# Another order of the steps in a fused layernorm, linear attention and Mish feed-forward kernel

## The chip, the cores and the metric

The kernel runs on one core of a Trainium2 chip. The metric is the device time of one execution in microseconds (us). A core has TensorE (PE, with its weight loads as PEld), VectorE (DVE), ScalarE (ACT), GpSimd (POOL) and SyncE (SP), each with its own instruction stream, and 16 DMA engines that work off what the queues of SP and ACT issue. All times below are in us from the start of the span unless another unit stands there.

## The reference

```python
x  = A_x                                   # [1, 2048, 448], bf16
xn = layernorm(x)                          # eps 1e-5, no scale or shift
# attention part, H = 16 heads of 28
q, k, v = heads(xn @ wqkv)                 # wqkv [448, 3*448]
pq = q @ w_phi[h];  pk = k @ w_phi[h]      # w_phi [16, 28, 28]
phi_q = concat(softmax(pq), softmax(-pq))  # 56 features a head
phi_k = concat(softmax(pk), softmax(-pk))
kv = phi_k^T v;   z = sum over tokens of phi_k
o  = (phi_q kv) / (phi_q z + 1e-6)
# feed-forward part, F = 1792
h   = xn @ w1 + b1
act = h * tanh(softplus(h))                # Mish
out = x + o @ wo + act @ w2
```

All tokens see the same kv and z, so no output of the attention part can be made before k and v of all tokens are done.

## The kernel before

Tokens are tiled 16 tiles of 128; tiles 2u and 2u+1 form pair u (u = 0 to 7). Almost all matmuls take 64 rows and run two at a time in the two halves of TensorE, one for each tile of a pair; each piece of such work is cut into a part 1 (8 matmuls of a projection) and a part 2 (6), which swap the halves.

The stages are these.

- *Weights of the feature maps.* Wq and Wk are loaded transposed, with one transposing DMA each (`lqT`, `lkT`, line 285), and their last 64 rows are copied once (`qda`, `kdd`). w_phi is loaded in two parts (line 301): 384 of its 448 rows (`lp0`) and the other 64 (`lp1`). POOL multiplies them with a mask into a block-diagonal Wbd (`bd`, line 547): the first two of three multiplies read the large part, the third the small one. PE multiplies WqT and WkT with Wbd (`wmq0` to `wmq3`, `wmk0` to `wmk3`, line 563), which gives the weights Wpq and Wpk that make pq and pk directly from xn. Each such group reads all of Wbd.
- *Layernorm.* Statistics of a tile on DVE (`st..d`, lines 468 and 469) or ACT (`st..a`, lines 460 to 464); rstd of a pair on ACT (`rs..a`, Ln and Exp, lines 481 and 483) or POOL (`rs..p`, lines 474 and 477); xn of a pair on DVE (`xn..d`, line 502) or POOL (`xn..p`, with a small shift on DVE, lines 490 and 497). Then xn is transposed on PE (`xt..a`, `xt..d`, `xt..b`, line 510) with the copy out of PSUM on ACT, DVE or half on each, or by a transposing DMA on SP's queue (`xt..m`, line 522). Such a DMA waits for xn of its pair, and for tiles 0 and 15 of x.
- *Projections.* `q`, `k`, `v` of each pair on PE (line 439). ACT makes exp of both signs from q (line 653) and k (line 592); v is copied by DVE or ACT (lines 517, 515). exp of q goes to one of three buffers (pair modulo 3) and is transposed per tile by DMA (`e0` to `e15`, line 661). exp of k is summed and inverted on DVE and normalised on POOL (`kn`, lines 600 to 604).
- *Key-value state.* `kv0` to `kv7` on PE (line 621) sum over all pairs; `kvz` on DVE (line 633) adds eps and masks with `mask2`, which POOL makes (`pk`, lines 351 to 360), and one transposing DMA hands it on as KVZ.
- *Feed-forward.* `f0.c` and `f1.c` are the two halves of the tokens for 14 blocks c of F; PE (line 439), then Mish on ACT (line 672), into rows of actT. The products with W2 are `G` in halves and `g` whole (lines 835, 797).
- *Output.* `nd` of a tile on PE (line 695), numerators and denominators on DVE (lines 710 to 721), the pair transposed by DMA (`ot..m`, line 730), and the product with Wo (`wo`, lines 835, 813). Both output products of a pair add up in the same two banks of PSUM; DVE adds x (line 762), SP stores (`sto`, `stt`).

What sets the order is one list of step names, ORDER. Each step appends its instructions to the streams of the engines it uses, in the order of the list; what an instruction must wait for is derived from what it reads and writes. So the list fixes the order on every engine and every queue, the bank of PSUM that a step gets, and, by a letter at the end of a name, the engine: a for ACT, d for DVE, p for POOL, s for SP's queue, m for a DMA, b for both.

```python
for name in order:
    steps[name]()
```

A load of x has `load_x(a, b, eng)` behind it: `x1` loads tiles 2 and 3, `x2` 4 and 5, `t6` and `t7` one tile, `x4` tiles 8 to 11, `x6` 12 to 15, `x0` 0 and 1. `lvm`, `ly0`, `ly1` load Wv, `l1m0` to `l1m2`, `lz0`, `lz1` W1, `l2` W2, `lo` Wo, `lb` b1. `z16` is 16 matmuls on constants ahead of everything on PE, `table` loads ACT's table, `pp`, `pi`, `pm`, `pv` are constants on POOL.

Of the kernel before, what the change touches and what calls it, by code (L numbers as in the profile page):

```python
# [146 lines left out]


ORDER = """
lp0a pp2 z16 lx1s pi pk st3d pp1 lqT lkT table lx2a pp0 pm lp1a st2d lba bd st4a rs1p st5d lx4a qda rs2a b1 xn1d wmq3a  # L150
xn2d lt6s lx0s wmq1a kdd wmq2a wmq0a xt1b xt2d wmk3a ly0s st6d lt7s st7d st9d wmk2a lvms wmk0a ly1s wmk1a q11 lx6s rs3a
xn3d q21 st8d st14d q12 rs4p xt3m q22 v21d st0d k21 xn4p st15d rs7p l1m2s e3 v11d v22a st11d v12a k22 st10d k11 st12d
xn7d v31d st13d xt4m st1d k12 k31 l1m0s pv q31 v32d rs0p e2 xt7m rs5a xn0d k32 k41 xn5d q32 e4 v41d k42 rs6p q41 xt0m
v42d xn6d k71 q42 k72 xt5m l1m1s v71a e6 xt6m kn2.1 v01a k01 lz0a v02d v72d kn1.1 k51 kn4.1 k02 e7 v51a k52 e5 lz1s k61
kn3.1 v52d kn1.0 k62 l2s q51 q61 q52 kn7.1 q62 f0.11 v61a f1.31 v62a e11 kn5.0 f0.12 kn6.1 f1.21 f1.11 f1.32 e12 e8
f1.22 kn6.0 kn0.1 f0.21 f1.12 e13 ep f0.22 f1.51 e10 f1.01 f0.121 f1.02 kv6 kv1 kn2.0 kn4.0 f0.122 f1.52 los f0.51 kn3.0
f0.71 kn7.0 f0.52 e9 f0.72 kn0.0 q71 q01 q72 q02 f0.101 kv2 kn5.1 kv0 kv7 e1 kv5 kv4 kv3 f1.61 kvz f0.102 e14 f1.121
f1.62 f1.122 f0.131 f0.61 f0.132 f0.31 e15 f1.71 f0.62 f0.32 f0.81 e0 f1.72 nd2 f0.82 f0.111 f0.01 f0.112 f0.41 nd3
f0.02 f0.42 f1.81 nd1 f0.91 ot1m f1.82 f0.92 f1.101 nd7 f1.91 f1.102 G11 nd0 f1.41 wo11 f1.92 nd6 G12 f1.111 wo12 f1.112
ot0m f1.42 ot3m nd5 G31 nd10 nd4 G01 wo32 G02 wo31 nd11 f1.131 G32 f1.132 ot5m nd14 ot2m wo01 G21 wo52 nd15 wo22 wo51  # L160
wo02 ot7m wob nd12 G51 wo21 nd13 G52 ot6m G42 sto1 G22 G41 sto0 nd9 nd8 wo61 G61 wo7F g14 G62 sto2 ot4m wo41 wo62 wo7H
sto3 wo42 sto5 stt14 sto4 sto6 g15 stt15
"""


# [816 lines left out]
```

## Time and profile before

| | us |
|---|---|
| three runs | 151.71, 152.47, 152.88 |
| median | 152.47 |
| profiled execution | 151.52 |
| its span, first to last instruction | 149.7 |
| PE busy | 144.5 |
| DVE busy | 103.0 |
| ACT busy | 71.6 |
| POOL busy | 38.7 |

The granted clock of TensorE was 1.0 over the whole span. The profile's busy rows show how much of each of 40 equal slices (3.7 us) an engine worked, in tenths. The chain of waits follows the work that ended last back from the end: what each piece waited for, or the piece before it on its engine. A row of the timeline has start, length, engine, line, operation, what it writes and reads, and how many instructions are merged into it; in brackets, how long the engine stood idle before it and what ended that. The rows of SPq and ACTq are the issues of DMAs; their landing times are in the view of the DMAs and of a tile. Times of merged rows reach from the first start to the last end.

### The profile page before, as it was taken

Reading aid. Unit: us, or ns where it says so; the run is one execution under the profiler, and the core shown is the slowest. Engines: PE = TensorE matmul, PEld = TensorE weight load, DVE = VectorE, ACT = ScalarE, POOL = GpSimd, SP = SyncE. Lnnn points to the kernel's source line nnn. Section 1 sums busy time; section 2 is a strip of 40 time slices with the busy share of each in tenths; the row PEclk is TensorE's granted clock in tenths of the full one; section 3 lists DMA queues with packets and bytes.
Section 4 is the critical chain, followed back from the end, with each engine's and each line's share of the span. In section 5 each row is a group of like instructions: output and inputs, shape, how many; then the busy total and the mean of one; then the engine's idle time right before and its main releaser. Section 6 shows DMA issues by size and latency. Waiting matters only on the chain.

```text
span 149.7 us, 3958 instructions
## 1 busy us (share of the span) xinstructions
PE 144.5 (97%) x1719; PEld 76.0 (51%) x1719; DVE 103.0 (69%) x228; ACT 71.6 (48%) x88; POOL 38.7 (26%) x55
## 2 busy tenths in 40 slices
PE   7989999799999999999999999999999999999991
PEld 2375554456555554744444455555555555554451
DVE  0689985849999992020179979799787996387072
ACT  3688989938999578986765612410020000000000
POOL 6800832044999999200000000000000000000000
PEclk9999999999999999999999999999999999999999
DMA  4994899999999990079300302300032112400604
GB/s 132 272 330 136 185 246 199 133 283 195 294 222 234 244 123 0 4 138 145 72 0 4 61 4 47 75 4 0 4 70 59 25 36 52 166 36 0 184 30 154
DMA packets 41484, 17.23 MB, mean 115 GB/s; under 512 B 35708, under 2 KB 40700, under 8 KB 41468
## 3 DMA queue, kind: packets, MB, share of 16 engines
q1 hardware_dynamic: 40448, 15.95, 50.6%
q10 hardware_dynamic: 1020, 1.04, 2.2%
q8 instruction: 13, 0.21, 0.6%
q14 instruction: 3, 0.02, 0.0%
HBM read 6.57 MB, written 1.84 MB: 56 GB/s over the span
## 4 chain that ended last, share of the span: by engine, by line
PE 86%; DMA 6%; DVE 3%; issue 1%; POOL 1%; ACT 0%; ACTq 0%
PE PS L439 45%; PE PS L835 31%; DMA xnT<-xn 3%; PE PS L797 3%; DMA Wraw<-in_A_w_phi_dram 3%; PE PS L695 2%; PE PS L621 2%; DVE xn L502 2%; PE PS L813 1%; PE PS L563 1%; POOL rstd L477 0%; PE PS L510 0%; DVE x_all L762 0%; ACT L317 0%; ACTq L301 0%
## 5 line engine op out<-in xcount | busy, mean ns | idle before, releaser
L439 PE MATMUL PS<-xnT,W 64*128 64x512 bf16 x392 | 45.0, 376 | 0.0
L672 ACT ACTIVATE actT<-PS,b1T 128x1024 bf16<-128x1024 f32 x28 | 29.9, 1112 | 30.7 <-PE PS L439 30.7
L835 PE MATMUL PS<-W,actT 64*128 64x448 bf16 x392 | 38.9, 349 | 0.0
L439 PEld LDWEIGHTS PS<-xnT,W 64*128 64x128 bf16 x392 | 19.2, 94 | 20.3 <-ACT actT L672 0.5
L604 POOL TENSOR_TENSOR actT<-actT,rSk 128x896 bf16<-128x896 bf16 x16 | 26.6, 1698 | 10.4 <-DVE rSk L602 10.4
L835 PEld LDWEIGHTS PS<-W,actT 64*128 64x128 bf16 x392 | 18.3, 94 | 17.7 <-issue 0.4
L600 DVE TENSOR_REDUCE Sk<-actT 128x32 f32<-128x896 bf16 x16 | 16.6, 1040 | 0.0
L762 DVE TENSOR_TENSOR x_all<-PS,x_all 128x448 bf16<-128x448 f32 (+1 forms) x16 | 9.1, 613 | 9.1 <-PE PS L835 8.7
L592 ACT ACTIVATE actT<-PS 128x896 bf16<-128x896 f32 x16 | 13.6, 929 | 3.4 <-PE PS L439 3.4
L710 DVE COPY Sq<-PS 128x16 f32<-128x16 f32 x32 | 4.0, 166 | 15.2 <-PE PS L695 15.2
L439 PE MATMUL PS<-Wv,xnT 64*128 64x448 bf16 x112 | 12.8, 349 | 0.8 <-DMA xnT<-xn 0.8
L439 PE MATMUL PS<-Wpk,xnT 64*128 64x448 bf16 x112 | 12.5, 349 | 0.0
L439 PE MATMUL PS<-Wpq,xnT 64*128 64x448 bf16 x112 | 11.8, 349 | 0.0
L468 DVE BATCH_NORM_STATS2 stats<-x_all 128x6 f32<-128x448 bf16 x15 | 9.1, 607 | 3.6 <-DMA x_all<-in_A_x_dram 3.5
L718 DVE TENSOR_TENSOR v_all<-v_all 128x464 f32<-128x464 f32 x16 | 10.3, 642 | 0.6
L714 DVE TENSOR_TENSOR v_all<-PS,Sq 128x464 f32<-128x464 f32 x16 | 10.3, 642 | 0.5
L721 DVE TENSOR_TENSOR xn<-v_all,rden 128x448 bf16<-128x448 f32 x16 | 10.0, 625 | 0.6
L716 DVE TENSOR_TENSOR v_all<-PS,Sq 128x464 f32<-128x464 f32 x16 | 10.1, 629 | 0.0
L653 ACT ACTIVATE actT<-PS 128x896 bf16<-128x896 f32 x10 | 8.5, 918 | 0.9 <-PE PS L439 0.9
L439 PEld LDWEIGHTS PS<-Wv,xnT 64*128 64x128 bf16 x112 | 5.8, 94 | 5.8 <-DVE rSk L602 1.2
L517 DVE CAST v_all<-PS 128x896 bf16<-128x896 f32 x5 | 5.3, 1077 | 4.7 <-PE PS L439 4.7
L439 PEld LDWEIGHTS PS<-Wpk,xnT 64*128 64x128 bf16 x112 | 5.9, 94 | 4.8 <-issue 0.3
(86 smaller groups left out, 123.9 us busy)
## 6 DMA issues: line engine op xcount, KB each, us to landing
W<-in_B_w_dram SPq DMA_DIRECT2D x1, 1568.0 KB, 8.8
out_dram<-x_all SPq DMA_DIRECT2D x7, 224.0 KB, 2.2
W<-in_B_w_dram SPq DMA_DIRECT2D x3, 448.0 KB, 4.1
Wo<-in_A_wo_dram SPq DMA_DIRECT2D x2, 336.0 KB, 3.4
x_all<-in_A_x_dram SPq DMA_DIRECT2D x2, 224.0 KB, 3.6
x_all<-in_A_x_dram ACTq DMA_DIRECT2D x1, 448.0 KB, 4.6
x_all<-in_A_x_dram SPq DMA_DIRECT2D x1, 448.0 KB, 4.5
Wv<-in_A_wqkv_dram SPq DMA_DIRECT2D x1, 336.0 KB, 4.5
```

The costliest lines, as they stand in the source:

```text
L439: ins = e.matmul(o, lhs(c, k), rhs(c, k), start=part == "1" and c == 0, stop=part == "2" and c == 2)
L468: op("DVE", lambda e: e.bn_stats(stats[:, t, :], x_all[:, t, :]), r=[("x", t)], w=[("st", t)], tag=f"bn{t}")
L592: op("ACT", lambda e, s=s: e.activation(E_of(u)[:, s, :, :], two(b, D), ACT.Exp, scale=1.0 if s == 0 else -1.0), r=[pb(b), pb(b + 1)], w=[ ...
L600: op("DVE", lambda e: e.tensor_reduce(Sk[u][:, s, :], Eh(), AX.X, ALU.add), r=[("E", u, s)], w=[("Sk", u, s)], tag=f"Sk{u}.{s}")
L604: op("POOL", lambda e: e.tensor_tensor(Eh(), Eh(), ap_on(rSk[u][:, s, 0:1], [[1, 2 * H], [0, DH]]), ALU.mult), r=[("E", u, s), ("rSk", u, ...
L672: op("ACT", lambda e: e.activation(actT[:, fc, q * 1024:(q + 1) * 1024], bank(b, 2), ACT.Mish, bias=b1T[:, fc:fc + 1]), r=[("b1T",), pb(b) ...
L714: op("DVE", lambda e: e.tensor_tensor(tv(t1[i]), num(0), sx(1), ALU.mult), r=[pb(b), pb(b + 1), ("Sq", i, 1)], w=[("t1", i)], tag=f"ta{t}")
L716: op("DVE", lambda e: e.tensor_tensor(tv(t2), num(1), sx(0), ALU.mult), r=[pb(b), pb(b + 1), ("Sq", i, 0)], w=[("t2",)], tag=f"tb{t}")
L718: op("DVE", lambda e: e.tensor_tensor(t1[i], t1[i], t2, ALU.add), r=[("t1", i), ("t2",)], w=[("t1", i)], tag=f"tc{t}")
L721: op("DVE", lambda e: e.tensor_tensor(o_sb[(t // 2) % 2][:, t % 2, :].rearrange("p (h d) -> p h d", d=DH), t1[i][:, :, 0:DH], ap_on(rden[i ...
L762: op("DVE", lambda e: e.tensor_tensor(x_all[:, t, 0:n], bank(b)[:, 0:n], x_all[:, t, 0:n], ALU.add), r=[pb(b), ("x", t)], w=[("out", t)], ...
L835: ins = e.matmul(bank(places[par][0])[:, 0:D], l, r, start=fresh[par], stop=places[par][2] and i >= len(todo) - 2)
```

## The change

The list is replaced by another one; nothing else changes. 17 step names differ, each in its engine letter only: statistics of tile 3 go from DVE to ACT and of tile 4 from ACT to DVE; rstd of pairs 1 and 0 from POOL to ACT and of pair 5 from ACT to POOL; xn of pairs 3 and 5 from DVE to POOL and of pair 4 from POOL to DVE; pair 1 is transposed on PE with the copy on ACT instead of half ACT, half DVE; `wmq3` and `wmk0` are copied by DVE instead of ACT, v of pair 7 by ACT instead of DVE (only the letter of a part 2 counts there, so the other changed letters of v do nothing); x's tiles 8 to 11 (`lx4`) and one tail of W1 (`lz0`) are loaded on SP's queue instead of ACT's. All else is order.

On ACT's queue the loads were large w_phi, x, small w_phi, b1, x, a tail of W1, and become small w_phi, x, b1, large w_phi. On SP's queue, behind `lx1 lqT lkT lt6`, there stood `lx0 ly0 lt7 lvm ly1 lx6`, then the first transposing DMA of xn (pair 3), and now `lvm ly0 lt7 lx4 ly1 lx6 lx0 lz0 l1m0`, then that DMA. The transposing DMAs of xn went 3, 4, 7, 0, 5, 6 and go 3, 4, 5, 7, 6, 0. On POOL `pk` moves from the start to behind all of `kn`.

```diff
--- before.py
+++ after.py
@@ -147,19 +147,19 @@
 
 
 ORDER = """
-lp0a pp2 z16 lx1s pi pk st3d pp1 lqT lkT table lx2a pp0 pm lp1a st2d lba bd st4a rs1p st5d lx4a qda rs2a b1 xn1d wmq3a
-xn2d lt6s lx0s wmq1a kdd wmq2a wmq0a xt1b xt2d wmk3a ly0s st6d lt7s st7d st9d wmk2a lvms wmk0a ly1s wmk1a q11 lx6s rs3a
-xn3d q21 st8d st14d q12 rs4p xt3m q22 v21d st0d k21 xn4p st15d rs7p l1m2s e3 v11d v22a st11d v12a k22 st10d k11 st12d
-xn7d v31d st13d xt4m st1d k12 k31 l1m0s pv q31 v32d rs0p e2 xt7m rs5a xn0d k32 k41 xn5d q32 e4 v41d k42 rs6p q41 xt0m
-v42d xn6d k71 q42 k72 xt5m l1m1s v71a e6 xt6m kn2.1 v01a k01 lz0a v02d v72d kn1.1 k51 kn4.1 k02 e7 v51a k52 e5 lz1s k61
-kn3.1 v52d kn1.0 k62 l2s q51 q61 q52 kn7.1 q62 f0.11 v61a f1.31 v62a e11 kn5.0 f0.12 kn6.1 f1.21 f1.11 f1.32 e12 e8
-f1.22 kn6.0 kn0.1 f0.21 f1.12 e13 ep f0.22 f1.51 e10 f1.01 f0.121 f1.02 kv6 kv1 kn2.0 kn4.0 f0.122 f1.52 los f0.51 kn3.0
-f0.71 kn7.0 f0.52 e9 f0.72 kn0.0 q71 q01 q72 q02 f0.101 kv2 kn5.1 kv0 kv7 e1 kv5 kv4 kv3 f1.61 kvz f0.102 e14 f1.121
-f1.62 f1.122 f0.131 f0.61 f0.132 f0.31 e15 f1.71 f0.62 f0.32 f0.81 e0 f1.72 nd2 f0.82 f0.111 f0.01 f0.112 f0.41 nd3
-f0.02 f0.42 f1.81 nd1 f0.91 ot1m f1.82 f0.92 f1.101 nd7 f1.91 f1.102 G11 nd0 f1.41 wo11 f1.92 nd6 G12 f1.111 wo12 f1.112
-ot0m f1.42 ot3m nd5 G31 nd10 nd4 G01 wo32 G02 wo31 nd11 f1.131 G32 f1.132 ot5m nd14 ot2m wo01 G21 wo52 nd15 wo22 wo51
-wo02 ot7m wob nd12 G51 wo21 nd13 G52 ot6m G42 sto1 G22 G41 sto0 nd9 nd8 wo61 G61 wo7F g14 G62 sto2 ot4m wo41 wo62 wo7H
-sto3 wo42 sto5 stt14 sto4 sto6 g15 stt15
+pp2 z16 pi lx1s lp1a lx2a st2d lba lqT lkT lt6s st5d lvms pm table lp0a st4d st3a rs1a xn1d rs2a xn2d pp1 bd qda ly0s b1
+wmq1a wmq0a wmq2a xt1a kdd lt7s lx4s ly1s lx6s lx0s wmq3d pp0 xt2d wmk1a wmk2a st6d wmk3a st7d wmk0d q11 rs3a lz0s xn3p
+st9d q21 l1m0s xt3m st8d rs4p st10d q12 st11d q22 v21d v11d xn4d k11 v12a k12 st12d lz1s rs5p k21 xt4m e3 xn5p xt5m
+st15d st0d st14d v22a l1m1s k22 st1d v31a rs0a k31 rs7p q31 xn7d v32d st13d k32 q32 v41d e2 xn0d k41 e5 v42d k42 rs6p
+xn6d k51 v51a xt7m k52 e4 xt6m xt0m v52d q51 q41 q52 kn5.1 kn4.1 l1m2s q42 e6 v71a k71 kn5.0 v72a e7 k72 pv l2s v61d
+v01d v62a kn3.1 k61 kn7.0 v02d kn2.1 k62 kn6.0 k01 kn7.1 q61 k02 f1.31 kn6.1 q62 e9 f1.21 f1.32 f1.22 kn2.0 e12 f1.11
+f0.11 f1.12 f0.12 f1.01 f0.121 kn1.1 e10 kn1.0 f0.21 f1.02 e11 kn0.1 f1.51 e8 f0.22 f0.51 f1.52 kn4.0 los f0.52 f0.71
+kn3.0 kv6 kv1 f0.72 q71 f0.122 q01 q72 ep e13 kv7 kn0.0 kv5 kv4 e15 kv2 kv0 kv3 pk f1.101 kvz e14 q02 f1.102 f0.91 f0.01
+f1.121 f0.92 f0.02 f0.81 f1.122 f0.82 nd2 f0.61 f1.71 f0.62 e1 nd1 f1.72 f0.101 f1.131 f0.131 f0.102 nd3 f1.132 f0.132
+e0 f1.61 nd0 ot1m f0.111 f1.62 f0.41 ot0m f0.112 f0.31 f0.42 wob nd4 f1.111 f0.32 nd5 f1.112 f1.91 wo11 G11 nd6 nd7 ot2m
+G12 f1.41 f1.92 wo12 f1.42 nd12 G21 wo01 ot3m wo21 nd13 ot6m G31 wo22 nd10 G22 G01 f1.81 nd9 wo32 f1.82 wo31 nd8 sto2
+G02 wo02 nd11 ot5m sto0 G32 nd15 ot4m G41 G51 nd14 G62 wo51 wo61 G61 ot7m wo41 wo7F g14 wo62 wo52 sto6 wo7H G52 G42 wo42
+stt14 sto5 sto4 sto3 g15 sto1 stt15
 """
```

## The prediction

> **What bounds the kernel now.** I read the page first, then the chain of waits, then the timeline of the first 40 us. The page says which engine sets the time: TensorE. Its 40 slices hold a 9 from the fourth to the last but one, except a 7 in the eighth.
>
> ```profile
> span 149.7 us, 3958 instructions
> PE 144.5 (97%) x1719; PEld 76.0 (51%) x1719; DVE 103.0 (69%) x228; ACT 71.6 (48%) x88; POOL 38.7 (26%) x55
> PE   7989999799999999999999999999999999999991
> ```
>
> The chain that ended last (start, length, what) says where the end is made outside PE's own work.
>
> ```profile
> 1.87 4.43 DMA Wraw<-in_A_w_phi_dram
> ...
> 6.97 0.72 POOL rstd L477
> ...
> 7.71 1.70 DVE xn L502 x6
> ...
> 9.46 0.56 PE PS L510 x7
> 10.03 0.93 PE PS L563 x16
> 10.96 10.91 PE PS L439 x114
> ...
> 24.52 5.23 DMA xnT<-xn
> ...
> 146.21 0.56 DVE x_all L762
> ```
>
> There are three pieces. A prelude runs to about 10.9: the small part of w_phi lands, POOL makes Wbd and the rstd of pair 1, DVE makes xn, PE transposes it and multiplies the weights. Then a body: the projections, FFN1 and both output products back to back on PE, with one stop, for the transposed pair 0 (24.52 plus 5.23: landed at 29.75). Then a tail from DVE's first sum after PE's last output (146.21) to 149.7. The change keeps every matmul, so the body's length stays. It can move three things: when the body starts, which stops lie in it, and the tail.
>
> **The start of the body.** These rows of the timeline (start, length, engine, line) are the prelude.
>
> ```profile
> 0.81 0.48 ACTq L301 DMA_DIRECT2D Wraw<-in_A_w_phi_dram  x1
> 1.24 2.03 SPq L285 DMA_TRANSPOSE WqT<-in_A_wqkv_dram  x1
> 1.32 1.28 ACT L317 ACT_TABLE_LOAD   x1 [1.32 <-PEq L967]
> 1.35 0.48 ACTq L269 DMA_DIRECT2D x_all<-in_A_x_dram  x1
> 1.87 0.53 ACTq L301 DMA_DIRECT2D Wraw<-in_A_w_phi_dram  x1
> 2.43 0.81 ACTq L304 DMA_DIRECT2D b_rows<-in_B_b_dram  x1
> 5.10 1.08 POOL L547 TENSOR_TENSOR Wbd<-Wraw,mask 128x280 bf16<-128x280 bf16 x2
> 6.37 0.33 POOL L547 TENSOR_TENSOR Wbd<-Wraw,mask 128x84 bf16<-128x84 bf16 x1 [0.18 <-DMA Wraw<-in_A_w_phi_dram]
> 7.31 1.09 PE L563 MATMUL PS<-Wbd,WqT 128*128 128x140 bf16 x16
> 9.87 1.09 PE L563 MATMUL PS<-Wbd,WkT 128*128 128x140 bf16 x16
> 10.89 2.82 PE L439 MATMUL PS<-Wpq,xnT 64*128 64x448 bf16 x28
> ```
>
> ACT's queue issues four loads in the order large w_phi (0.81), x, small w_phi (1.87), b1 (2.43). The change makes that small w_phi, x, b1, large w_phi. So what left the chain's first link is the small part, and what enters it is the large one. The table load does not hold up issues (x went out at 1.35 under the load that began at 1.32), so the large part goes out when b1's issue ends: b1 starts at 1.87 now, and with 0.53 to 0.81 for its issue the large part starts at 2.4 to 2.7; I take 2.5. When does it land?
>
> ```profile
> DMA to landing us min/median/max: 2.9/3.7/4.4
> WkT<-in_A_wqkv_dram SPq DMA_TRANSPOSE x1, 5.9
> x_all<-in_A_x_dram ACTq DMA_DIRECT2D x1, 448.0 KB, 4.6
> ```
>
> The first row is Wraw's two loads: 4.4 is the small part (the chain's 4.43), so 2.9 is the large one, issued before any transposing DMA. In its new place it is in flight with both transposing DMAs, as the small part was. Lower bound 2.9, upper bound the 5.9 of a transposing DMA itself. I take 4.4, from the row that it is nearest to in place, and the 448 KB of x on the same queue with 4.6 says that size adds little. So it lands at 6.9 (5.4 to 8.4).
>
> The Trainium skill, "DMA: Bandwidth & Descriptors", section "Queues, rings and completion order", says that each DMA engine takes turns between its queues, a packet of typically 9 to 17 descriptors at a time. By that rule, as an estimate, the large part's 384 rows, 24 an engine, would be two or three packets where the small part's four rows are one, so it would wait two or three times as long for its turns, and the sum would come out near that of the second rival below. The trace only half agrees: 448 KB of x landed in 4.6.
>
> Behind the landing stand all three Wbd multiplies, since the large part feeds the first two and POOL's order keeps the third behind them: 1.08 + 0.33 = 1.41, and 0.07 to notice the landing (1.87 + 4.43 is 6.30, the third multiply began at 6.37). Before, the first two were done while the small part was still under way; that cover is gone. Then PE: four Wq groups 1.09, two transposes of 0.56, four Wk groups 1.09: 3.30 in all before the first projection, in both orders. The body starts at 6.9 + 0.07 + 1.41 + 3.30 = 11.7 (10.2 to 13.2). It cannot start before 7.31 + 3.30 = 10.6, because PE came to the Wq matmuls at 7.31 straight from the warm-up and the bias transpose, which stay. Before it was 10.89. **Term 1: +0.8 (-0.3 to +2.3).**
>
> The rest of the prelude I cost at nothing. Pair 1's rstd goes from POOL (0.72 behind Wbd) to ACT, whose Ln and Exp need no Wbd, so xn leaves the chain: the wait for Wbd covers it now. Wq's last evacuation moves to DVE, behind the copy for WkT; PE needs it only with the first projection, and if the body could start at 10.6 it would be next in line.
>
> **The stops in the body.** Rows of the timeline, and the landing times of the transposing DMAs of xn:
>
> ```profile
> 12.39 0.29 ACT L481 ACTIVATE lnv<-mv,eps_col 128x2 f32<-128x2 f32 x1 [0.24 <-DVE mv L469]
> 13.94 1.75 SPq L522 DMA_TRANSPOSE xnT<-xn  x1
> 16.22 1.73 POOL L497 TENSOR_SCALAR xn<-x_all,rstd,shift 128x448 bf16<-128x448 bf16 x3 [0.51 <-DVE shift L490]
> 26.43 1.09 DVE L517 CAST v_all<-PS 128x896 bf16<-128x896 f32 x1 [1.85 <-PE PS L439]
> 27.43 0.88 DVE L502 TENSOR_SCALAR xn<-x_all,mv,rstd 128x448 bf16<-128x448 bf16 x3
> 29.88 0.93 PE L439 MATMUL PS<-Wv,xnT 64*128 64x448 bf16 x8 [0.81 <-DMA xnT<-xn]
> ...
> DMA to landing us min/median/max: 2.9/4.7/5.2
> ```
>
> The stop for pair 0 is the 0.81 in the sixth row. The new order takes the pairs 1, 2, 3, 4, 5, 7, 6, 0 instead of 1, 2, 3, 4, 7, 0, 5, 6, so pair 0 is needed later: 246 matmuls of the projections stand ahead of its first one, at 10.91/114 = 0.096 each 23.5, so PE is there at 11.7 + 23.5 = 35.2. Its transposing DMA stands on SP's queue behind pair 6's, which waits for xn of pair 6, which waits on DVE behind the evacuation of v of pair 4: 148 matmuls, 25.9, then 1.09 and 0.88, so 27.9; an issue of 1.8 (the 13.94 row) puts pair 0's DMA at 29.7, and 5.2 puts its landing at 34.9. That is 0.3 to spare. **Term 2: -0.8.**
>
> What may be late next is pair 3. Its xn moves from DVE to POOL. Its rstd on ACT began at 12.39, behind DVE's statistics of tiles 6 and 7, which follow the transposes and so come 0.8 later: 13.2. Ln, Exp and the shift take 0.7 (13.94 less the 0.88 of an xn and 12.39), POOL's xn 1.73: the DMA goes out at 15.6 instead of 13.94. It also waits for tiles 0 and 15, and behind tile 0's load SP's queue now has a tail and a third of W1, all loads that wait for nothing and are issued well before. PE needs pair 3 after 84 matmuls instead of 78, at 11.7 + 8.0 = 19.7. By the shortest landing it is there at 18.5, by the median at 20.3; before, PE did not stop for it at 10.89 + 7.5 = 18.4, so its landing took 4.4 at most, and that gives 20.0. Pair 4 is next on SP as before and is needed after 126 matmuls instead of 120. Pair 5 is needed after 154, at 26.4; on POOL two rstd of 0.9 (an estimate: 0.72 and a smaller one) and 1.73 follow 15.6, 19.1, and behind pair 4's issue and with 5.2 it lands near 26. **Term 3: +0.2 (0 to +1.0).** If the body starts early, this term grows, since pair 3's loads don't come earlier with it.
>
> **Further back.** These rows are the normalising of phi(k) on POOL, the mask that moves behind it (first and last of six instructions), and the hand-over to the output part.
>
> ```profile
> 1.93 0.14 POOL L351 MEMSET mask<- 128x56 f32 x1
> 3.32 0.53 POOL L360 MEMSET KVT<- 128x512 uint32 x1
> ...
> 35.73 24.89 POOL L604 TENSOR_TENSOR actT<-actT,rSk 128x896 bf16<-128x896 bf16 x15 [4.25 <-DVE rSk L602]
> ...
> 63.38 1.38 DVE L633 SCALAR_TENSOR_TENSOR KVT<-PS,epsT,mask 60x448 bf16<-60x448 f32 x2 [6.28 <-PE PS L621]
> KVZ<-KVT SPq DMA_TRANSPOSE x1, 4.9
> 74.28 0.26 DVE L710 COPY Sq<-PS 128x16 f32<-128x16 f32 x2 [9.52 <-PE PS L695]
> ...
> 76.75 0.62 DVE L721 TENSOR_TENSOR xn<-v_all,rden 128x448 bf16<-128x448 f32 x1
> ...
> Wpk<-xn SPq DMA_TRANSPOSE x2, 2.9
> ```
>
> POOL's mask for KVT moves from the start (1.93 to 3.85, 1.9) to behind the last normalising. POOL takes 24.89/15 = 1.66 for each of 16, 26.6. The first can start when k of pair 5 is through (176 matmuls, 28.5, and about 3 for exp and sums, an estimate), at 32, so they end near 59 and the mask near 61. PE's key-value products were through at 63.38, when kvz began; ahead of them now stand 14 matmuls less, so 62: the mask has 1 to spare. kvz 1.4 and its transposing DMA 4.9 give 68.3, and between there and the first output product stand 76 matmuls instead of 98, so it comes at 62 + 76 x 10.9/98 = 70.4 instead of 74. The cover shrinks from 4.3 to 2; what is past it costs one for one. DVE, idle for 9.52 before that product, starts 4 earlier on the same 16 products. Their new order ends with pair 7, not pair 4. Behind its last product PE has 80 matmuls, 7.7, before it needs the pair transposed: 3.1 on DVE (74.28 to 77.37) and 2.9 in the DMA leave 1.7. FFN1's order, Mish and the stores I cost at nothing: PE has the same blocks, ACT idles between them. **Term 4: 0 (0 to +0.3:** three stores now stand close ahead of the last tile's, where there were two).
>
> **Sum.** Against the profiled 151.52 (span 149.7 and 1.8 around): 0.8 - 0.8 + 0.2 + 0 = +0.2, so 151.7; all lower ends -0.3 - 0.8 = -1.1, all upper ends 2.3 - 0.8 + 1.0 + 0.3 = +2.8. The profiled run lies 0.95 under the median of the runs, 152.47. On the median's scale: 152.7 (151.4 to 155.3).
>
> **Rivals.**
> *w_phi in time.* The large part lands by 5.8, and the body starts at 10.6: -1.1, 151.4. For it: 2.9 is what it took alone. Against: its neighbours on the queue took 4.4 and 4.6 beside the transposing DMAs. Even so it is less than 1%.
> *w_phi late: slower.* One place: POOL waits for the large part, PE stands still behind the warm-up. Each microsecond of landing past 5.8 costs one; from 8.2 on the total is over 1% slower (+2.1 at the start, -0.8, +0.2). With six times the rows it may meet two or three times the small part's delay of 4.4 - 2.9 = 1.5; then it lands at 2.5 + 2.9 + 3 to 4.5 = 8.4 to 9.9, and the time is 154.2 to 155.7. The packet rule of the Trainium skill named above would give this. For it: no load of so many short rows was in flight beside the transposing DMAs before. Against: the 4.6 of x, though in fewer rows. Its harshest form is a delay that goes by rows, 1.5 for 64, so 9 for 384: landing 14.4, the body at 19.2, about 160.
> *A pair or an exp buffer late.* Pair 3, 5 or 0 lands after 5.2; or the exp of q of pair 5 on ACT waits for its buffer, which pair 2 leaves only with its second transpose, now behind pair 7's on SP: 1 to 1.5 instead of 0.2, 153.7.
> *The new order does nothing that counts:* the loss at the start and the removed stop cancel; this is the middle of my forecast and has its time.
>
> **Chances.** Forecast (landing 5.8 to 8.2) 0.51; in time 0.16; late 0.18; late by rows 0.05; a pair or a buffer 0.10. About 1%, 1.5, is what a measurement of this kernel can tell from no change. Faster by over 1% needs the early case and a measurement 0.4 below it: 0.10. Slower: most of the late case 0.15, by rows 0.05, a third of the last 0.03, the forecast's upper edge 0.04: 0.27. Same: 0.63. I give 152.7 and the range 151.2 to 155.2: it leaves out the rows case, the late case's end and some of the early case's spread, below 0.2 together.
>
> **What would show it.** Right: Wbd on POOL waits for w_phi until near 7, PE idles about 1 between the warm-up and Wq, the projections start near 11.7, and no stop over 0.3 follows. The first step is wrong if PE goes on at 7.3; the second and third if PE waits for pair 0, 3 or 5; the fourth if DVE waits for POOL's mask or PE for KVZ. A body that is longer or shorter than before by more than its stops would show that equal matmuls don't cost the same in the new order; the sum has no term for that.

## The result, and the profile after

The changed kernel is slower. Its median is 156.62 us (6 runs, 155.65 to 157.35) against 151.57 for the kernel before (6 runs, 151.22 to 152.88): a ratio of 1.0308, 95% interval 1.0253 to 1.0364. The profiled execution took 156.84 with a span of 155.1, against 151.52 and 149.7.

The page of the changed kernel: span, PE's busy time, then PE's busy tenths and the granted clock over 40 slices of 3.9 us.

```profile
span 155.1 us, 3959 instructions
PE 144.9 (93%) x1719; PEld 76.9 (50%) x1719; DVE 102.1 (66%) x226; ACT 72.6 (47%) x89; POOL 39.6 (26%) x56
PE   7507999999999999999999999999999999999993
PEclk9985799999999999999999999999999999999999
```

PE is busy for 144.9, as before (144.5). What is new is at the left edge: a slice with next to no matmul, and three slices in which the clock was not granted in full. The chain of waits of the changed kernel (start, length, what) tells what PE stood still for.

```profile
2.96 8.24 DMA Wraw<-in_A_w_phi_dram
11.38 0.58 issue
11.96 0.76 POOL Wbd L547 x2
12.77 1.51 PE PS L563 x12
...
16.21 1.52 PE PS L563 x16
17.73 43.05 PE PS L439 x436
...
152.06 0.56 DVE x_all L762
```

The large part of w_phi is the chain's first link, as the prediction had it, but it landed at 2.96 + 8.24 = 11.20, not at 6.9. The chain then names nothing but PE up to DVE's last sums: the wait for pair 0 (24.52 + 5.23 before) is gone. These rows of the timeline are the prelude.

```profile
0.82 0.54 ACTq L301 DMA_DIRECT2D Wraw<-in_A_w_phi_dram  x1
1.27 2.15 SPq L285 DMA_TRANSPOSE WqT<-in_A_wqkv_dram  x1
1.40 0.59 ACTq L269 DMA_DIRECT2D x_all<-in_A_x_dram  x1
2.96 0.40 ACTq L301 DMA_DIRECT2D Wraw<-in_A_w_phi_dram  x1
3.47 6.25 SPq L285 DMA_TRANSPOSE WkT<-in_A_wqkv_dram  x1
11.13 0.16 PE L666 MATMUL PS<-ident,b_rows 14*128 14x14 bf16 x1 [5.27 <-DMA b_rows<-in_B_b_dram]
11.34 1.37 POOL L547 TENSOR_TENSOR Wbd<-Wraw,mask 128x280 bf16<-128x280 bf16 x3 [8.42 <-DMA Wraw<-in_A_w_phi_dram]
17.66 2.82 PE L439 MATMUL PS<-Wpq,xnT 64*128 64x448 bf16 x28
```

The body starts at 17.66 instead of 10.89. PE idled 5.27 before the bias transpose, because b1's load was late too, and 1.47 more for Wbd. WkT's issue took 6.25 on SP's queue, where it had taken 2.49. So not one load was late but all that were in flight behind the small part of w_phi, which still landed in 4.6 (4.4 before). The landing times of the changed kernel (KB each, us from issue to landing):

```profile
x_all<-in_A_x_dram ACTq DMA_DIRECT2D x1, 224.0 KB, 9.5
Wraw<-in_A_w_phi_dram ACTq DMA_DIRECT2D x1, 21.0 KB, 8.2
WqT<-in_A_wqkv_dram SPq DMA_TRANSPOSE x1, 10.0
WkT<-in_A_wqkv_dram SPq DMA_TRANSPOSE x1, 9.0
```

The same loads in the kernel before, beside the 5.9 of WkT:

```profile
x_all<-in_A_x_dram ACTq DMA_DIRECT2D x1, 224.0 KB, 3.1
Wraw<-in_A_w_phi_dram ACTq DMA_DIRECT2D x1, 21.0 KB, 2.9
WqT<-in_A_wqkv_dram SPq DMA_TRANSPOSE x1, 5.5
```

The busy times by stretch end in the granted clock, the DMA engines' busy share (above 1 means that more than one transfer was under way on an engine) and GB/s. First the changed kernel, then the kernel before.

```profile
3.00:5.00 2.00, 2.00 (x9) 0.83 (x8) 0.81 (x2) 1.96 (x4) 0.00 (x0) 1.00 1.20 124
5.00:7.00 2.00, 0.86 (x4) 0.20 (x2) 0.00 (x0) 1.39 (x5) 0.00 (x0) 1.00 1.24 112
7.00:9.00 2.00, 0.00 (x0) 0.00 (x0) 0.00 (x0) 0.00 (x0) 0.00 (x0) 1.00 1.34 102
9.00:11.00 2.00, 0.00 (x0) 0.00 (x0) 0.12 (x1) 0.00 (x0) 0.00 (x0) 0.87 1.31 111
11.00:13.00 2.00, 0.40 (x4) 0.34 (x4) 1.86 (x6) 0.25 (x1) 1.62 (x4) 0.50 1.19 335
```

```profile
3.00:5.00 2.00, 2.00 (x6) 0.68 (x5) 1.36 (x4) 0.52 (x2) 1.77 (x7) 1.00 1.15 270
5.00:7.00 2.00, 2.00 (x7) 0.67 (x5) 1.02 (x4) 1.37 (x6) 1.66 (x6) 1.00 1.26 266
7.00:9.00 2.00, 1.70 (x24) 1.39 (x24) 1.46 (x6) 1.82 (x6) 0.68 (x1) 1.00 1.08 364
```

From 3 to 11 us the engines were as busy as before and moved 102 to 124 GB/s, where the kernel before moved 266 to 364 from 3 to 9. I call that a jam: more work in the queues would not explain fewer bytes. And when PE came back the granted clock was 0.50, so its prelude, from 12.77 to 17.66, took 4.89 where the prediction had added up 3.30.

The ledger of the span, +5.4: start +6.77; stop for pair 0 -0.81; body without stops, up to DVE's sums after PE's last output, 134.4 against 134.5, so -0.1; from there to the end 3.0 against 3.5, so -0.45.

### The profile page after: what moved, and what is told of

It is laid out like the page before. It is cut to its first block, busy times and chain, and to the rows that moved or that the text cites. A ratio compares the mean times of both kernels' runs of the same rounds, so it can differ in the third digit from the quotient of the medians.

```text
span 155.1 us, 3959 instructions
## 1 busy us (share of the span) xinstructions
PE 144.9 (93%) x1719; PEld 76.9 (50%) x1719; DVE 102.1 (66%) x226; ACT 72.6 (47%) x89; POOL 39.6 (26%) x56
## 4 chain that ended last, share of the span: by engine, by line
PE 90%; DMA 5%; ACTq 1%; issue 1%; POOL 1%; DVE 0%; ACT 0%; POOLq 0%
PE PS L439 48%; PE PS L835 30%; DMA Wraw<-in_A_w_phi_dram 5%; PE PS L797 3%; PE PS L695 2%; PE PS L563 2%; PE PS L621 2%; PE PS L510 1%; PE PS L813 1%; ACTq L304 1%; POOL Wbd L547 1%; ACTq L269 0%; DVE x_all L762 0%; ACTq L301 0%; DVE x_all L783 0%
## 5 line engine op out<-in xcount | busy, mean ns | idle before, releaser
L439 PEld LDWEIGHTS PS<-xnT,W 64*128 64x128 bf16 x392 | 18.3, 94 | 21.2 <-ACT actT L672 0.6
L835 PEld LDWEIGHTS PS<-W,actT 64*128 64x128 bf16 x392 | 19.2, 94 | 15.9
L468 DVE BATCH_NORM_STATS2 stats<-x_all 128x6 f32<-128x448 bf16 x15 | 9.1, 609 | 10.1 <-DMA x_all<-in_A_x_dram 10.0
L716 DVE TENSOR_TENSOR v_all<-PS,Sq 128x464 f32<-128x464 f32 x16 | 10.1, 629 | 0.0
L439 PEld LDWEIGHTS PS<-Wpk,xnT 64*128 64x128 bf16 x112 | 5.4, 94 | 5.1 <-ACT actT L653 0.2
L439 PEld LDWEIGHTS PS<-Wpq,xnT 64*128 64x128 bf16 x112 | 5.3, 94 | 5.3 <-ACT actT L672 0.3
```

What stands on the lines that cost most here:

```text
L439: ins = e.matmul(o, lhs(c, k), rhs(c, k), start=part == "1" and c == 0, stop=part == "2" and c == 2)
L468: op("DVE", lambda e: e.bn_stats(stats[:, t, :], x_all[:, t, :]), r=[("x", t)], w=[("st", t)], tag=f"bn{t}")
L716: op("DVE", lambda e: e.tensor_tensor(tv(t2), num(1), sx(0), ALU.mult), r=[pb(b), pb(b + 1), ("Sq", i, 0)], w=[("t2",)], tag=f"tb{t}")
L835: ins = e.matmul(bank(places[par][0])[:, 0:D], l, r, start=fresh[par], stop=places[par][2] and i >= len(todo) - 2)
```

## The experiments

The trace also has each DMA packet. Counted by microsecond and size, x's tiles 4 and 5 are 128 packets of 1792 bytes on ACT's queue, and the transposing DMAs are 256-byte packets on SP's. With nothing else under way 1025 to 1130 of the latter start in a microsecond.

```
packets that start     before                  changed
in us                transposing    x       transposing    x
2 to 3                    0          7           42          0
3 to 4                  334        121          434         10
4 to 5                  891          0          232         26
5 to 6                 1025          0          353         18
6 to 7                 1029          0          277         16
7 to 8                  305          0          263         22
8 to 9                    0          0          182         20
9 to 10                   0          0          306         14
10 to 11                  0          0          413          2
11 to 12                  0          0         1082          0
```

Before, x's packets were out before 4.0 and the first transposing one started at 3.45: they met for half a microsecond. In the changed kernel the first transposing packet started at 2.83 and x's at 3.54; from there both crawled, until x was through at 10.1. The runs had to say what part of the new order does this, and what else it costs.

### Old order of ACT's loads in the new list

```diff
- pp2 z16 pi lx1s lp1a lx2a ... table lp0a st4d
+ lp0a pp2 z16 pi lx1s lx2a lp1a ... table st4d
```

> The changed order, but ACT's queue issues its four early loads as before: large w_phi, x, small w_phi, b1. Theory (the large part of w_phi, 384 short rows, in flight beside the two transposing DMAs, slows every DMA that is in flight with it): WqT and WkT land near 6.7 and 9.2 again, no granted clock below 1.0, the projections start at 10.6 to 10.9 instead of 17.7, and the time is 150.0 to 151.5. Rival (the rest of the new order does it: x on SP's queue, xn on POOL, other places of the loads): the transposing DMAs still land after 10 and the time stays above 155.

Measured: 152.61 (10 runs), ratio to before 1.0043 (1.0004 to 1.0081). x landed in 3.1, WqT in 5.1; the body started at 10.24, and the granted clock did not fall. So the four issues on ACT's queue carry nearly all of the loss. What is left are stops in the body, rows of its timeline:

```profile
13.38 1.69 PE L439 MATMUL PS<-Wv,xnT 64*128 64x448 bf16 x16 [0.31 <-issue]
19.88 0.93 PE L439 MATMUL PS<-Wv,xnT 64*128 64x448 bf16 x8 [1.03 <-ACT v_all L515]
32.74 3.35 ACT L653 ACTIVATE actT<-PS 128x896 bf16<-128x896 f32 x4 [2.22 <-DMA EqT<-actT]
36.15 1.50 PE L439 MATMUL PS<-Wv,xnT 64*128 64x448 bf16 x14 [0.69 <-ACT actT L653]
```

They add up to 2.03. In the third row ACT waits 2.22 for the exp buffer that pair 2 leaves with its second transposing DMA, and 0.69 of it reaches PE.

### New order of ACT's loads in the old list

```diff
- lp0a pp2 z16 lx1s ... table lx2a pp0 pm lp1a st2d lba bd
+ lp1a pp2 z16 lx1s ... table lx2a pp0 pm st2d lba lp0a bd
```

> The order before, but ACT's queue issues small w_phi, x, b1, large w_phi, then its other loads. Theory (large w_phi beside the transposing DMAs): x on ACT's queue, WqT, WkT and the large part all land between 9 and 12.5, the projections start near 17 to 18, the time is 156 to 158. Rival (the rest of the new order does it): WqT and WkT land near 6.7 and 9.2, and only the wait for the large part is added, 1 to 3 us, so 152.5 to 154.5.

Measured: 157.36 (4 runs), ratio 1.0366 (1.031 to 1.0422); the body started at 16.60. Its landing times:

```profile
x_all<-in_A_x_dram ACTq DMA_DIRECT2D x1, 224.0 KB, 7.7
Wraw<-in_A_w_phi_dram ACTq DMA_DIRECT2D x1, 21.0 KB, 6.8
WqT<-in_A_wqkv_dram SPq DMA_TRANSPOSE x1, 8.2
```

The order of four loads makes the whole loss without any other part of the change.

### Short rows, or long ones, behind b1

Two kernels, each the kernel before with one more load on ACT's queue behind b1, which nothing reads: 384 rows of 56 bytes, and 384 of 512 bytes.

```diff
+    add("extra", lambda: dma("ACT", lambda e: e.dma_start(Xtra[:, :, :], ...), ...))
- ... lba bd st4a
+ ... lba extra bd st4a
```

> The kernel before with one more load on ACT's queue behind b1: the same 384 rows of w_phi, 56 bytes each, into a tile that nobody reads. The large part itself stays first in the queue. Theory (short rows beside the transposing DMAs): WqT lands near 10, WkT near 12, projections start 5 to 7 us later, time 156 to 158. Rival (it was the place of the large part, that is x and b1 ahead of it and its reader waiting, not what it does to others): WqT and WkT land near 6.7 and 9.2, time within 0.5 of before.

> As the run before it, but the extra load has the same number of rows, 384, of 512 bytes each (a piece of W1, not read by anyone). If the number of rows beside the transposing DMAs counts: as slow as with the 56-byte rows, WkT after 11. If the shortness of the rows counts: WqT and WkT land within 1 us of 6.7 and 9.2 and the time is within 1 us of before.

Measured, one run each: 151.76 and 151.90; WqT in 5.3 and 5.6, WkT in 4.8 and 5.3, body from 10.75 and 10.89. My first theory, that many short rows beside the transposing DMAs make the jam, falls. These rows moved after x was through, the 56-byte ones beside WkT's packets (915 to the microsecond from 6 to 7), the 512-byte ones largely in the pause between WqT's last packet (5.72) and WkT's first (6.29).

### x first on ACT's queue, the large part still last

```diff
- pp2 z16 pi lx1s lp1a lx2a
+ lx2a lp1a pp2 z16 pi lx1s
```

> The changed order with x (tiles 4 and 5) first on ACT's queue: x, small w_phi, b1, large w_phi. Large w_phi stays late. Theory (the 128 rows of x, 1792 bytes each, start on the DMA engines after the transposing packets have begun, and the two streams then slow each other): x lands near 3.5, WqT near 6.5, WkT near 9, large w_phi near 7, granted clock 1.0, projections start at 10.5 to 12, time 150.5 to 153. Rival (the small part ahead of the large one, or the late large one, does it): WkT lands after 11 and the time is above 155.

Measured: 152.80 (10 runs), ratio 1.0061 (1.0029 to 1.0093); clock 1.0, x in 4.1, WqT in 5.9. The small part is still early and the large part last, and there is no jam. This is the case that the prediction had priced; its timeline:

```profile
2.70 0.40 ACTq L301 DMA_DIRECT2D Wraw<-in_A_w_phi_dram  x1
7.07 1.40 POOL L547 TENSOR_TENSOR Wbd<-Wraw,mask 128x280 bf16<-128x280 bf16 x3 [4.15 <-DMA Wraw<-in_A_w_phi_dram]
11.27 2.82 PE L439 MATMUL PS<-Wpq,xnT 64*128 64x448 bf16 x28
19.89 0.93 PE L439 MATMUL PS<-Wv,xnT 64*128 64x448 bf16 x8 [0.46 <-DMA xnT<-xn]
33.58 3.35 ACT L653 ACTIVATE actT<-PS 128x896 bf16<-128x896 f32 x4 [3.05 <-DMA EqT<-actT]
36.98 1.31 PE L439 MATMUL PS<-Wv,xnT 64*128 64x448 bf16 x12 [0.69 <-ACT actT L653]
```

The large part landed in 4.2, at 6.9, and the body started at 11.27. The stops were 1.70: 0.46 for pair 3, 0.20 for another pair, 1.04 for ACT behind the exp buffer.

### x later in the old list: fourth, then third

```diff
- lp0a ... lx2a pp0 pm lp1a st2d lba bd
+ lp0a ... pp0 pm lp1a st2d lba lx2a bd
+ lp0a ... pp0 pm lp1a lx2a st2d lba bd
```

> The order before with x (tiles 4 and 5) moved behind b1 on ACT's queue: large w_phi, small w_phi, b1, x. Both parts of w_phi come first, as good as before. Theory (x's rows behind the first transposing packets slow both): WqT lands after 8, WkT after 10.5, x after 8, time above 154.5. Rival (w_phi's place counts): WqT and WkT land near 6.7 and 9.2, x lands by 7.5, time below 153.

> The order before with x (tiles 4 and 5) third on ACT's queue: large w_phi, small w_phi, x, b1. x is issued about 0.5 later, near 1.85, behind the issue of WqT's transposing DMA by 0.6 instead of 0.1, with w_phi as good as before. Theory (what counts is whether x's rows reach the DMA engines before WqT's transposing packets; if not, the two share the engines and both crawl): WqT lands after 8, WkT after 10.5, x after 7, time above 154.5. Rival (the small part as first load of the queue does it): WqT, WkT near 6.7 and 9.2, time below 153.

Measured: fourth 153.54 (2 runs), ratio 1.0109 (1.0022 to 1.0196), x in 4.0, WqT in 5.4, WkT in 5.5, body from 13.35; third 153.40 in the profiled run and 155.91 in a second one that left no profile, x in 5.1, WqT 6.0, WkT 5.4, body from 13.14. The expected long jam did not come in the profiled runs. But they hardly put the theory to the test: third, x's first packet (4.80) came when 1648 of WqT's 1792 packets were out, fourth (4.84) when 1732 were, so x met WqT's last packets and not its first. The second run with x third had a mean granted clock of 0.975, near the changed kernel's 0.978; whether it had a jam isn't known. In both PE lost its time to x's late tiles (ACT's copy of WqT stands behind tile 4's statistics) and to a granted clock of 0.50 afterwards.

### x in rows of half the length

x's tiles 4 and 5 as two loads of 448-byte rows, in the changed kernel.

> The changed order, with x (tiles 4 and 5) at its new place as two DMAs of 256 rows of 448 bytes instead of one of 128 rows of 1792 bytes. If the length of the rows is what does not go together with the transposing packets: WkT lands before 10 and the time is below 154. If any rows of that many bytes do it: WkT lands after 11 and the time is above 155.

Measured, one run: 154.08; x in 6.2, WqT in 7.3, body from 14.63. The jam is shorter though there are four times the packets: x's took 3.9 instead of 6.6, and 424 transposing packets started in a microsecond meanwhile instead of 266. The length of the rows seems to have a part in it, by this one run, but isn't all of it.

### A longer warm-up on PE

```diff
- pp2 z16 pi
+ pp2 z40 pi
```

> The changed order with 40 instead of 16 warm-up matmuls, so that PE works until the late landings and the granted clock does not fall. DMA is as slow as in the changed kernel (WkT near 12.5). If the clock has its share of the loss: the prelude's matmuls from the first Wq group to the first projection take 3.3 instead of 4.9, and the time is 1.4 to 1.8 below the changed kernel, near 155.0. If it has none: 156.6.

Measured: 154.74 (2 runs), ratio 1.0188 (1.0098 to 1.0278). The clock did not fall and the prelude took 3.09 (11.76 to 14.85) instead of 4.89. Those 1.8 are the clock's; with x first and with WqT later (below) the same matmuls took 2.74 and 2.75 at the full clock, so it may be 2.1. The body started another 1.0 earlier because the large part landed at 10.2 in this execution; that this comes from the warm-up isn't shown, and the medians lie 1.9 apart. The jam itself, x in 8.3 and WqT in 8.9, is as it was: it needs no idle PE.

### WqT's DMA half a microsecond later

```diff
- pp2 z16 pi lx1s lp1a ... qda ly0s b1
+ pp2 z16 pi lx1s ly0s lp1a ... qda b1
```

> The changed order with one small load of Wv (56 KB) issued on SP ahead of WqT's transposing DMA, so that this one is issued near 1.85, after x's 1.40. ACT's queue stays as in the changed order: small w_phi, x, b1, large w_phi. Theory (x before WqT's packets is good): x lands by 5, WkT by 10, granted clock 1.0, projections start at 11 to 12.5, time 152 to 153.5. Rival (small w_phi first does it): WkT after 11, time above 155.

Measured: 152.68 (8 runs), ratio 1.0054 (1.0019 to 1.0088). WqT went out at 1.88 instead of 1.27; x, issued at 1.40 as in the changed kernel, landed in 4.3, WqT in 6.2, WkT in 5.2.

```profile
x_all<-in_A_x_dram ACTq DMA_DIRECT2D x1, 224.0 KB, 4.3
WqT<-in_A_wqkv_dram SPq DMA_TRANSPOSE x1, 6.2
12.36 2.82 PE L439 MATMUL PS<-Wpq,xnT 64*128 64x448 bf16 x28
```

ACT's queue is that of the changed kernel, and the jam is gone. The body started at 12.36, and its stops were 0.86.

### WqT's DMA first, in the kernel before

ACT's queue as before; on SP's, WqT ahead of x's tiles 2 and 3. Then the same with the extra load of 56-byte rows behind b1.

```diff
- lp0a pp2 z16 lx1s ... pp1 lqT lkT
+ lqT lp0a pp2 z16 lx1s ... pp1 lkT
```

> The kernel before with WqT's transposing DMA first on SP's queue, ahead of x's tiles 2 and 3; the order on ACT's queue is the old one. Theory (what counts is that x's 1792-byte rows on ACT's queue enter just behind WqT's first packets): WqT goes out at 0.8 instead of 1.24, so x, still issued at 1.35, now meets its packets: x takes over 6 instead of 3.1, WqT over 8 instead of 5.5, and the time is over 154. Rival (the small part of w_phi at the head of ACT's queue is needed for the jam): x stays near 3 to 4, WqT near 5.5 to 6; tiles 2 and 3 come later behind WqT, so the body starts 1 to 2 later and the time is 152 to 153.5.

> The kernel before with WqT's transposing DMA first on SP's queue and, behind b1 on ACT's queue, an extra load of 384 rows of 56 bytes that nothing reads. Without the extra load x took 4.3 and WqT 5.7 in this place. Theory (short rows behind x lengthen the jam): x over 5.5, WqT over 7. Rival: x 4.3 and WqT 5.7 as without it, within 0.5.

Measured without the extra load: 155.24 (2 runs), ratio 1.0227 (1.0057 to 1.0397). The landing times:

```profile
x_all<-in_A_x_dram ACTq DMA_DIRECT2D x1, 224.0 KB, 4.3
WqT<-in_A_wqkv_dram SPq DMA_TRANSPOSE x1, 5.7
```

Both landing times of the theory were missed. Its time, over 154, came, but not by these landings; the rival had WqT right, and x and the time too low. This is the run that put x well behind WqT's first packets (551 of them were out) and got no long jam: while x's packets were in flight (3.3 to 5.1) the transposing ones went at 336 a microsecond, not far from the changed kernel's 266, but x passed in 1.8. So "x behind WqT's first packets" is not enough for a jam of 7 us. The rest of the loss is tiles 2 and 3 behind WqT, which held DVE and with it Wbd, and the clock (0.50 from 11.5 on): body from 14.55. With the extra rows x took 5.0 and WqT 6.2, between the two expectations, though the extra rows themselves moved only after x was through (5.8); the time is 157.33 (2 runs, ratio 1.0389, 1.0266 to 1.0513), with the body from 15.10 and a stop of 1.25.

### Where the large part of w_phi stands

In the changed kernel: the large part ahead of x on ACT's queue, then the large part on SP's queue between WqT and WkT.

```diff
- lx1s lp1a lx2a st2d lba lqT lkT ... table lp0a
+ lx1s lp1a lp0a lx2a st2d lba lqT lkT ... table
+ lx1s lp1a lx2a st2d lba lqT lp0s lkT ... table
```

> The changed kernel with the order small part, large part, x, b1 on ACT's queue: the 384 rows of 56 bytes go out at 1.40, where x stood, and x near 1.9. Theory (long rows meeting WqT's first packets jam): the large part lands within 5, x meets WqT's packets 0.5 later than in the changed kernel and the jam is short, as with x third in the old order (x 5, WqT 6): the time is 153 to 154. Rival (any load of 100 rows and more at that place jams, or the place behind the small part does it): large part over 7, WqT over 8, time over 155.

> The changed kernel with the large part of w_phi on SP's queue between WqT's and WkT's transposing DMAs; ACT's queue keeps small part, x, b1, issued at the same times, and WqT too. Theory (the jam is long where the 384 short rows are on ACT's queue behind x while x meets WqT's packets, and short without them): x lands within 5 and WqT within 6.5, as with x third in the old order (5.1 and 6.0). Rival (where the first packets of x and WqT meet sets the length by itself): x over 7 and WqT over 8, as in the changed kernel, and the time over 155.

Measured, large part second: 154.76 (2 runs), ratio 1.0195 (0.9953 to 1.0437); the large part in 6.6, x in 6.5, WqT in 7.7: between the two expectations. Within this one run the packets tell the two loads apart: while only 56-byte rows were under way on ACT's queue (3.0 to 4.0) 739 transposing packets started in a microsecond, once x's 1792-byte rows came (4.3 to 7.9) 295.

Large part on SP's queue: 156.45 (2 runs), ratio 1.0331 (1.0209 to 1.0454). The landing times:

```profile
x_all<-in_A_x_dram ACTq DMA_DIRECT2D x1, 224.0 KB, 8.7
WqT<-in_A_wqkv_dram SPq DMA_TRANSPOSE x1, 9.2
```

The jam is the changed kernel's, with nothing behind x on ACT's queue but b1. The rival's numbers came: the large part's rows on ACT's queue don't make its length.

### Two attempts at a better kernel

The first is the new list with ACT's old loads, and pair 2's second exp transpose ahead of pair 7's DMA on SP's queue. The second is the old list with pair 1's rstd on ACT and v of pair 7 ahead of pair 0's.

```diff
- v51a xt7m k52 e4 xt6m        (new list, ACT's old loads)
+ v51a e4 xt7m k52 xt6m
```

```diff
- bd st4a rs1p ... v01a k01 lz0a v02d v72d     (old list)
+ bd st4a rs1a ... v72d v01a k01 lz0a v02d
```

> The changed order with ACT's old order of early loads (the first experiment) and pair 2's second transpose of exp moved ahead of pair 7's transposing DMA on SP. If the exp buffer of pairs 2 and 5 makes the stop at 36.15 there (0.69): that stop goes, the sum of PE's stops falls from 2.0 to about 1.3, and the time falls by about 0.7, to 151.9. If ACT is late anyway: the stop stays within 0.2.

> The order before with two moves taken from what the runs showed: rstd of pair 1 on ACT instead of POOL behind Wbd, and the second half of pair 7's v ahead of pair 0's first half on PE, in the stop for pair 0. If the two terms of the prediction (start of the body by xn, stop for pair 0) are sized right: the body starts at 10.5 to 10.7 instead of 10.9, the stop of 0.8 shrinks to 0.3 or less, and the time is 0.5 to 0.9 below before, near 151.0. If other waits are next in line: within 0.3 of before.

Measured: 152.05 (10 runs), ratio 1.0011 (0.9974 to 1.0048), and 152.31 (12 runs), ratio 1.0031 (0.9999 to 1.0063). In the first the stop for the exp buffer went and one of 1.83 for a pair's DMA, now behind e4, came at 33.65; ACT still waited 2.05. In the second the body started at 10.32, as expected, and PE then stopped 2.20 for pair 0; its profiled execution was its longest (154.37), so the size of that stop isn't relied on. Neither beats the kernel before.

### What the runs say together

Packets of x's tiles 4 and 5 and of the transposing DMAs, in us, one profiled execution each. The fourth column counts the transposing packets (1792 for each of WqT and WkT) that were out before x's first; the fifth those that started in a microsecond while both were under way, that is from the later of the two first packets to x's last.

| kernel | first transposing packet | x, first to last | out before x's first | per us with x | WqT landed in | body from |
|---|---|---|---|---|---|---|
| before | 3.45 | 2.72 to 3.99 | 0 | 605 | 5.5 | 10.89 |
| x first | 3.49 | 2.04 to 4.00 | 0 | 353 | 5.9 | 11.27 |
| WqT later | 3.85 | 2.98 to 4.62 | 0 | 451 | 6.2 | 12.36 |
| x third, old list | 2.93 | 4.80 to 6.21 | 1648 | 128 | 6.0 | 13.14 |
| WqT first, old list | 2.19 | 3.31 to 5.09 | 551 | 336 | 5.7 | 14.55 |
| large part second | 2.81 | 4.30 to 7.93 | 985 | 295 | 7.7 | 14.42 |
| new loads, old list | 2.69 | 3.54 to 8.35 | 472 | 332 | 8.2 | 16.60 |
| large part on SP | 2.70 | 3.64 to 9.52 | 514 | 281 | 9.2 | 17.10 |
| changed | 2.83 | 3.54 to 10.13 | 390 | 266 | 10.0 | 17.66 |

In the last five rows x starts well inside WqT's packets, and 266 to 336 of them start in a microsecond instead of about 1100. The first three rows say less: there the two overlap for 0.5 to 0.8 only, at the start of the transposing, where fewer packets start anyway (318 and 309 in the first half microsecond with x third and fourth, before x was under way).

What differs in the last five rows is how fast x itself gets through. Ahead of the first transposing packet it needs 1.3 to 2.0, behind it 1.4 to 6.6. Shown is that the jam goes when x's packets are put ahead (by ACT's order, or by WqT's issue), and that neither the large part's rows on ACT's queue nor the rest of the new list make it. What stays open is what sets x's own rate behind the transposing packets: 128 packets in 1.8 with WqT first in the old list, in 6.6 in the changed kernel, though x met WqT there after 551 and here after 390 of its packets. The slow runs have the small part of w_phi at the head of ACT's queue, but no run changed that part alone; the quick one also has a load of x's tiles between WqT and WkT on SP's queue, which no slow run has.

## Why the prediction was wrong

**What bounds the kernel** held: PE's body without stops is 134.4 against 134.5, and only start, stops and tail moved.

**Term 1** failed, +6.77 where it had +0.8 and at most +2.3. The landing took 8.24 instead of 4.4, the prelude on PE 4.89 instead of 3.30, and the load went out at 2.96 instead of 2.5. The step is "Lower bound 2.9, upper bound the 5.9 of a transposing DMA itself". Both bounds are rows of one order, in which x had left before the transposing packets came; I read them as properties of the transfers. The change moved x's packets from 0.7 ahead of the first transposing packet to 0.7 behind it. The diff shows nothing of the kind at that place: x is second on ACT's queue before and after, and its issue moved from 1.35 to 1.40. I had followed the large part alone ("what entered is the large one"), and of x only its landing time. With x ahead, the estimate is good: x first on ACT's queue landed the large part at 6.9, as predicted, and the body came at 11.27 for 11.7.

The second half of the failure is that "3.30 in all before the first projection, in both orders" assumed the full clock. After 5.27 of idling the granted clock was 0.50 and the same matmuls took 4.89. The longer warm-up shows that 1.8 to 2.1 of these are the clock's. The Trainium skill, "TensorE: Matmul & The Clock Gate", Part 1 on the clock gate, says that PE drops to half its clock after an idle window of about 3.4 us and is back after a busy one; the changed kernel agrees (no matmul from 7.08 to 10.49, and 0.50 from there), but other runs had their clock halved without such a window (last section).

A floor of the same term is wrong too: "It cannot start before 7.31 + 3.30 = 10.6". The 16 warm-up matmuls don't take a fixed time. In the kernel before they start 0.43 apart until 6.36 and 0.22 apart from then on, and end at 7.17; in the changed kernel the step comes at 3.67, and they end at 5.86. The clock's row shows 1.0 for that stretch, but by the spacing PE ran at half its pace until then. And 3.30 adds up rows that overlap: without long waits and at the full clock the prelude took 2.72 to 3.09. With the large part first, two kernels with the new list and one with the old one started the body at 10.24, 10.15 and 10.32.

**Term 2**, -0.8, was right: no stop for pair 0 in the changed kernel, nor in any run with the new order behind the prelude.

**Term 3**, +0.2, came out at 0 in the changed kernel, its lower end, and for a reason I had not: with the body at 17.66 every pair's DMA had time. Where the jam is cured, it was mis-sized: the new stops are 2.03 with ACT's old loads, 1.70 with x first and 0.86 with WqT later. Most of it is not pair 3 but the exp buffer that pair 2 leaves (ACT waits 2.2 to 3.1) and ACT's v. The buffer was named, as a rival with a chance of 0.10 and a price of 1 to 1.5.

**Term 4** held in its waits. kvz on DVE waited for PE's products and not for POOL's mask, PE waited neither for KVZ nor for an output pair, and the tail became 0.45 shorter where I had 0 to +0.3; what shortened it isn't shown.

**The rivals.** "w_phi late" has the right place, POOL waiting for the large part and PE standing still behind the warm-up, and of the prices I gave the nearest, 154.2 to 155.7; it still falls short by the clock, and its reason is refuted. Six times the rows was the argument: 384 such rows beside the transposing DMAs cost nothing behind b1. By the packet rule of the Trainium skill named there one queue's load waits while the engines work off the packets of another. That alone is not what the trace shows: the engines moved 102 to 124 GB/s instead of 266 to 364, and the transposing DMAs were late as well. "The new order does nothing that counts" is what the runs without the jam come near: 1.0043, 1.0061 and 1.0054.

So the range, 151.2 to 155.2, was too low at the top by 1.4, and the miss of the sum is larger than that: +5.05 against the kernel before (156.62 and 151.57) where it had +0.2. The forecast case was given 0.51 although its main row came from a neighbour in another order.

## What to carry to other kernels

A landing time is a property of what was in flight at once, not of the transfer. When the order of issues changes around a transposing DMA, list for every load whether its packets leave before or after that DMA's first ones, those of loads that keep their place in their queue too: 0.6 us of one issue decided 5.3 of the start here. Price a late start of PE with its idle time's effect on the granted clock, and before trusting a reorder, undo the order of the first few loads alone; that one run found most of the loss.

## What was unexpected of the hardware

- A plain load of 128 rows of 1792 bytes on ACT's queue cuts the transposing DMAs on SP's queue from about 1100 packets of 256 bytes in a microsecond to some 300, and can itself take 6.6 instead of 1.3. In the changed kernel both together then move 102 to 124 GB/s with busy shares of 1.2 and more. 56-byte rows do it far less (739 packets from 3 to 4 with the large part second, 923 with x third).
- The load and WqT were issued at nearly the same times before (1.35 and 1.24) and after (1.40 and 1.27), yet x's first packet came 0.8 later and WqT's 0.6 earlier. The order of ACT's four loads sets this: 2.98 and 3.58 with the old order in the new list, 3.54 and 2.69 with the new order in the old one. By what way isn't shown, and issue times don't tell.
- The clock was halved in some runs after a shorter idle time than in the changed kernel, and not in others after a longer one: with x fourth it went to 0.50 at 8.8, after PE had idled since 6.8, with WqT later an idle 2.92 cost nothing. The idle time alone doesn't tell. In all traces the clock changes only at whole steps of 3.41 us, counted from its first rise. PE was busy for 0 to 44% of the step ahead of nine of the ten halvings before the last outputs, and for 52% or more of every step after which the clock stayed at 1.0, but for one: with x in rows of half the length it stayed after 44% and fell after 51%. So one idle time can count or not, by how the steps cut it. With x fourth PE was busy for 41% of the step from 5.4 to 8.8; with WqT later the idle time fell on two steps, busy for 55% and 53%.
